# Modulation rows of an adaLN block: from one-column matmuls on TensorE to float32 sums on VectorE

## The chip, the cores and the metric

The kernel runs on one core of a Trainium2 chip. The metric is the device time of one execution in microseconds (us). Each kernel was executed several times; I quote the median of its runs. Where it matters I give the mean clock that the chip granted to TensorE beside the time, as time/clock.

Engines are abbreviated as in the profile: PE is TensorE (the matmuls), PEld its weight loads, DVE VectorE, ACT ScalarE, POOL GpSimd. "L255" in a profile line is line 255 of that kernel's source, so the same function has different line numbers before and after.

## The reference, cut to what matters

```python
# S=2048, D=1024, F=3584, 32 heads of 32
mod = silu(c) @ w_mod                      # (1, 6*1024): six rows
sa, ca, ga, sb, cb, gb = mod.reshape(6, D)
h = layernorm(x) * (1 + ca) + sa
x = x + ga * attention(h, wqkv, wo)        # linear attention, phi(t) = where(t > 0, t+1, exp(t)) + 1e-6
h = layernorm(x) * (1 + cb) + sb
x = x + gb * ((silu(h @ w_gate) * (h @ w_up)) @ w_down)
```

The rows `sa` and `ca` are needed at once. The four "late" rows are not: `ga` is wanted when `wo` is used, `sb` and `cb` at the second layernorm, `gb` at the very end.

## The kernel before

The 2048 rows of x are handled in four row blocks of 512. The program is one hand-made list of stages, each of eight "groups" of eight 128x512 matmuls. A label names a group: `("K", 2, 0)` is the first group of the K projection of row block 2. Code hung on a label with `put` is emitted behind that group. The early stages run in this order:

K0 → V0 → KV0 → Q0 → K1 → V1 → KV1 → K2 → V2 → KV2 → K3 → V3 → KV3 → Q1, Q2, Q3 and attention output → gate/up (GU) and down (D).

A KV stage is two halves of 16 matmuls, and the first group of the next stage stands between the halves, so that PE has something to do while the last V group is evacuated.

```python
def nextbank():                     # five PSUM banks, in turn
    b = bank[state["b"]]; state["b"] = (state["b"] + 1) % 5; return b

def phi_to(dst, acc):               # K and Q groups: one ACT and two DVE operations
    nc.scalar.activation(out=e, in_=acc, func=ACT.Exp)
    nc.vector.tensor_scalar(out=e, in0=e, scalar1=1.0, scalar2=PHI_EPS, op0=ALU.min, op1=ALU.add)
    nc.vector.scalar_tensor_tensor(out=dst, in0=acc, scalar=0.0, in1=e, op0=ALU.max, op1=ALU.add)

def v_group(sc_, t, h):             # V groups: evacuated by ACT alone
    ...                             # eight matmuls into acc
    nc.scalar.copy(out=v_c[...], in_=acc)

def ln(st):                         # layernorm of one 128-row tile
    ln_stats(st)                    # DVE statistics, GpSimd power
    ln_xn(st, True)                 # GpSimd normalises
    nc.sync.dma_start_transpose(out=M4[...], in_=xns[st % 6])

def modulate(sc_, cc, sT, c1T):     # h * (1 + ca) + sa on DVE, 128x512
    nc.vector.tensor_scalar(out=h, in0=h, scalar1=c1T[:, cc:cc+1], scalar2=sT[:, cc:cc+1], ...)

def late_mm(i):                     # half a late row: 32 one-column matmuls on PE
    for ii in range(4):
        for j in range(8):
            nc.tensor.matmul(mps[:, col:col+1], lhsT=wml[i % 3][:, j, ii*P:(ii+1)*P], rhs=scT[:, j:j+1], ...)

def late_bc(q, dst):                # a row broadcast to 128 partitions, for ga and gb
    ...                             # DVE writes rep, PE multiplies it with the identity, ACT copies

for sc in (2, 3):                   # row blocks 2 and 3: four tiles, then two times four modulates
    put_ln(sc, [("K", sc-1, 1), ("K", sc-1, 3), ("K", sc-1, 5), ("K", sc-1, 7), ("V", sc-1, 4), ("V", sc-1, 6)])
lab = [(k, sc, i) for sc in (1, 2) for k in ("K", "V") for i in (2, 6)]
for i in range(8):
    put(lab[i], lambda i=i: late_mm(i))
...
put(("K", 2, 0), lambda: nc.sync.dma_start(out=wo, in_=wo_v))     # 2 MB
```

Of the kernel before, what the change touches and what calls it, by code (L numbers as in the profile page):

```python
# [8 lines left out]
ACT = mybir.ActivationFunctionType  # L9
ALU = mybir.AluOpType  # L10
BF16 = mybir.dt.bfloat16
F32 = mybir.dt.float32
# [9 lines left out]
def kernel(  # L22
# [13 lines left out]
    nc = tc.nc  # L36
    P = nc.NUM_PARTITIONS
    _, S, D = A_x.shape
# [3 lines left out]
    DC = D // P  # L42
# [4 lines left out]
    STC = SCW // P  # L47
    NB = 512
    NH = D // NB
# [13 lines left out]
    wo_v = A_wo.rearrange("(c p) n -> p c n", p=P)  # L63
# [3 lines left out]
    wm_v = w_mod.rearrange("(p j) n -> p j n", j=DC)  # L67
    c_v = c.rearrange("o (p j) -> p (o j)", j=DC)

    const = ctx.enter_context(tc.tile_pool(name="const", bufs=1))  # L70
# [6 lines left out]
    bank = [psum.tile([P, NB], F32, name=f"bank{i}") for i in range(8)]  # L77
# [3 lines left out]
    M3 = const.tile([P, 16384], BF16, name="M3")  # L81
    M4 = const.tile([P, NSC, DC, SCW], BF16, name="M4")
    M5 = const.tile([P, 14336], BF16, name="M5")
# [3 lines left out]
    def view(region, off, shape, dtype=BF16):  # L87
        n = 1
        for s_ in shape:
            n *= s_  # L90
        w = n * (2 if dtype == F32 else 1)
        ap = region[:, off:off + w]
        if dtype == F32:
            ap = ap.bitcast(F32)
        if len(shape) == 2:
            ap = ap.rearrange("p (a b) -> p a b", a=shape[0])
        elif len(shape) == 3:
            ap = ap.rearrange("p (a b c) -> p a b c", a=shape[0], b=shape[1])
        return ap
# [8 lines left out]
    wml = [view(M3, 4096 * (1 + i), [DC, NB]) for i in range(3)]  # L108
# [9 lines left out]
    wo = view(M6, 0, [DC, D])  # L118
    x1rs = [view(M6, 2048 * i, [D], F32) for i in range(2)]
    obs = [view(M6, 4096 + 1024 * i, [D]) for i in range(2)]  # L120
    yts = [view(M6, 6144 + 1024 * i, [NB], F32) for i in range(2)]
    xs = [view(M7, 1024 * i, [D]) for i in range(6)]
    xns = [view(M7, 6144 + 1024 * i, [D]) for i in range(6)]
    wgs = [view(M7, 4096 * i, [DC, FBW]) for i in range(3)]
# [11 lines left out]
    def load_x(st):  # L136
        nc.sync.dma_start(out=xs[st % 6], in_=x2[st * P:(st + 1) * P, :])
# [22 lines left out]
    load_wk(6, 7)  # L160
    load_wk(7, 8)

    zt = const.tile([P, NB], BF16, name="zt")
    nc.vector.memset(zt[:], 0.0)
    ident = const.tile([P, P], BF16, name="ident")
    make_identity(nc, ident[:])
    neg_half = const.tile([P, 1], F32, name="neg_half")
# [4 lines left out]
    saT = const.tile([P, DC], BF16, name="saT")  # L172
    ca1T = const.tile([P, DC], BF16, name="ca1T")
    sbT = const.tile([P, DC], BF16, name="sbT")
    cb1T = const.tile([P, DC], BF16, name="cb1T")
    m1 = const.tile([P, 6, DC], BF16, name="m1")
    ga_bc = const.tile([P, D], BF16, name="ga_bc")
    gb_bc = const.tile([P, D], BF16, name="gb_bc")
    KVZ = const.tile([P, HG, KVW], BF16, name="KVZ")
    rep = const.tile([P, DC, P], BF16, name="rep")  # L180

    scT = const.tile([P, DC], BF16, name="scT")
    nc.scalar.activation(out=scT[:], in_=c_sb[:], func=ACT.Silu)

    def warm(n):
        for _ in range(n):
            nc.tensor.matmul(bank[7][:], lhsT=zt[:, 0:P], rhs=zt[:], start=True, stop=True)


    stat = {}  # L190
# [25 lines left out]
    def ln(st):  # L216
        ln_stats(st)
        ln_xn(st, True)
        sc_, t = divmod(st, STC)
        nc.sync.dma_start_transpose(out=M4[:, sc_, :, t * P:(t + 1) * P], in_=xns[st % 6])  # L220

    def modulate(sc_, cc, sT, c1T, c0=0, c1=SCW):
        h = M4[:, sc_, cc, c0:c1]
        nc.vector.tensor_scalar(out=h, in0=h, scalar1=c1T[:, cc:cc + 1], scalar2=sT[:, cc:cc + 1],  # L224
                                op0=ALU.mult, op1=ALU.add)


    state = {"b": 0}

    def nextbank():  # L230
        b = bank[state["b"]]
        state["b"] = (state["b"] + 1) % 5
        return b
# [51 lines left out]
                                    in1=mask[:, P:KVW].unsqueeze(1).to_broadcast([P, n, HPC]), op=ALU.mult)  # L285


    LATE = [(2, "ga"), (3, "sb"), (4, "cb"), (5, "gb")]

    def load_late(i):  # L290
        q, kb = LATE[i // 2][0], i % 2
        k0 = q * D + kb * NB
        nc.sync.dma_start(out=wml[i % 3], in_=wm_v[:, :, k0:k0 + NB])

    def late_mm(i):
        q, kb = LATE[i // 2][0], i % 2
        mps = bank[7][:, 320 + 8 * q:328 + 8 * q]
        for ii in range(NB // P):
            col = kb * (NB // P) + ii
            for j in range(DC):  # L300
                nc.tensor.matmul(mps[:, col:col + 1], lhsT=wml[i % 3][:, j, ii * P:(ii + 1) * P],  # L301
                                 rhs=scT[:, j:j + 1], start=False, stop=(j == DC - 1), skip_group_check=True)
        if kb == 1:
            nc.vector.tensor_copy(out=m1[:, q, :], in_=mps[:, 0:DC])

    def late_fin(q):
        if q == 3:
            nc.vector.tensor_copy(out=sbT[:], in_=m1[:, 3, :])
        elif q == 4:
            nc.vector.tensor_scalar_add(out=cb1T[:], in0=m1[:, 4, :], scalar1=1.0)  # L310
        else:
            nc.vector.tensor_copy(out=rep[:], in_=m1[:, q, :].unsqueeze(2).to_broadcast([P, DC, P]))

    def late_bc(q, dst):
        for h in range(NH):
            b = nextbank()
            for i in range(NB // P):
                cc = h * (NB // P) + i
                nc.tensor.matmul(b[:, i * P:(i + 1) * P], lhsT=rep[:, cc, :], rhs=ident[:], start=True, stop=True)
            nc.scalar.copy(out=dst[:, h * NB:(h + 1) * NB], in_=b[:])  # L320


    def tr0(st):
# [25 lines left out]
    def mod_pair(p):  # L349
        mod_mm(0, 2 * p, 2 * p + 2)  # L350
        mod_mm(1, 2 * p, 2 * p + 2)
        mod_rows(2 * p, 2 * p + 2)

    warm(21)
    for st in range(STC):
        ln_stats(st)
    mask = const.tile([P, KVW], BF16, name="mask")
# [6 lines left out]
    ln_xn(0, False)  # L364
    tr0(0)
    warm(3)
    ln_xn(1, False)
    tr0(1)
# [13 lines left out]
    for cc in range(2):  # L382
        modulate(0, cc, saT, ca1T, 0, 2 * P)
    G = [(t, h) for t in range(STC) for h in range(NH)]
    for cc in range(2):
        for g in range(4):
            kmm(bank[g], 0, G[g][0], G[g][1], cc)
        if cc == 0:
            tr0(3)
            tr0_evac(3)  # L390
            for c_ in range(2):
                modulate(0, c_, saT, ca1T, 2 * P, 4 * P)
    for cc in range(2):
        for g in range(4, 7):
            kmm(bank[g], 0, G[g][0], G[g][1], cc)
        if cc == 0:
            mod_pair(1)
            for c_ in range(2, 4):
                modulate(0, c_, saT, ca1T)
# [25 lines left out]
    def put(label, *fns):  # L425
        after.setdefault(label, []).extend(fns)
# [143 lines left out]
                    add(("D", st, 1), lambda st=st: d_mm(st, 1))  # L570


    def put_ln(sc_, labels):
        for t in range(STC):
            put(labels[t], lambda t=t: ln(sc_ * STC + t))
        for i in range(2):
            put(labels[STC + i],
                lambda i=i: [modulate(sc_, cc, saT, ca1T) for cc in range(4 * i, 4 * i + 4)])

    put_ln(1, [("V", 0, 1), ("V", 0, 2), ("V", 0, 3), ("V", 0, 4), ("Q", 0, 2), ("Q", 0, 3)])  # L580
    for sc in (2, 3):
        put_ln(sc, [("K", sc - 1, 1), ("K", sc - 1, 3), ("K", sc - 1, 5), ("K", sc - 1, 7),
                    ("V", sc - 1, 4), ("V", sc - 1, 6)])
    put(("V", 0, 6), lambda: load_late(0), lambda: load_late(1), lambda: load_late(2))
    put(("V", 0, 7), lambda: [load_x(st) for st in range(8, 12)])
    put(("V", 1, 7), lambda: [load_x(st) for st in range(12, 16)])


    lab = [(k, sc, i) for sc in (1, 2) for k in ("K", "V") for i in (2, 6)]
    for i in range(8):  # L590
        put(lab[i], lambda i=i: late_mm(i))
        if i + 3 < 8:
            put(lab[i], lambda i=i: load_late(i + 3))
    put(("K", 1, 7), lambda: late_fin(2))
    put(("V", 1, 1), lambda: late_bc(2, ga_bc))
    put(("V", 1, 7), lambda: late_fin(3))
    put(("K", 2, 0), lambda: nc.sync.dma_start(out=wo, in_=wo_v))
    put(("K", 2, 7), lambda: late_fin(4))
    put(("V", 2, 7), lambda: late_fin(5))
    put(("K", 3, 1), lambda: late_bc(5, gb_bc))  # L600
    for cc in range(DC):
        put(("V", 3, cc), lambda cc=cc: nc.vector.tensor_tensor(out=wo[:, cc, :], in0=wo[:, cc, :], in1=ga_bc[:],
                                                               op=ALU.mult))


# [78 lines left out]
```

## Time and profile before

| | before |
|---|---|
| median time (four runs) | 847.24 us |
| span of the profiled run (a fifth one, 847.73 us), mean PE clock | 845.9 us, 1.00 |
| PE busy | 833.4 us, 99% |
| DVE busy | 322.9 us, 38% |
| ACT busy | 144.8 us, 17% |

The profile's first part (busy time and share of the span, with the number of instructions) and its fourth (the chain of work that ended last, by engine), before:

```profile
PE 833.4 (99%) x4368; PEld 395.7 (47%) x4452; DVE 322.9 (38%) x617; ACT 144.8 (17%) x270; POOL 78.8 (9%) x142
...
PE 95%; DVE 1%; SPq 1%; DMA 1%; issue 1%; ACT 0%; DVEq 0%
```

PE is the bound, and hardly ever waits.

The timeline of PE before, through the V1 and KV1 stages (start, duration, engine, source line, operation, count; in brackets the idle time before and what ended it):

```profile
74.10 0.94 PE L301 MATMUL bank<-scT,M 128*128 128x1 bf16 x32
74.90 1.89 PE L242 MATMUL bank<-M,M 128*128 128x512 bf16 x7
76.62 3.62 PE L257 MATMUL bank<-M,M 128*128 128x512 bf16 x16
81.22 0.62 PE L319 MATMUL bank<-ident,rep 128*128 128x128 bf16 x8 [0.98 <-DVE rep L312]
...
93.64 1.07 PE L274 MATMUL bank<-M 128*128 128x129 bf16 x16
94.55 1.89 PE L242 MATMUL bank<-M,M 128*128 128x512 bf16 x8
96.28 1.07 PE L274 MATMUL bank<-M 128*128 128x129 bf16 x16
```

L242, L257 and L274 are K, V and KV matmuls. L301 is a batch of 32 one-column products for half a late row: the group behind it starts 0.80 us after it. L319 is the broadcast of `ga`; PE even waits 0.98 us for the data. At 94.55 stands K2's first group, 1.73 us of work, between the halves of KV1.

The timeline of DVE before, in the same stretch:

```profile
80.48 0.68 DVE L312 COPY rep<-m 128x1024 bf16<-128x1024 bf16 x1
90.06 2.67 DVE L224 TENSOR_SCALAR M<-M,ca1T,saT 128x512 bf16<-128x512 bf16 x8 [8.89 <-DMA M<-M]
```

DVE has nothing to do for 8.89 us, waiting for the last DMA transpose of row block 2, and then modulates all of the block in 2.67 us. The eight modulated slices are ready at 92.7, before K2 wants them at 94.55. DVE's wait costs nothing, because no V group needs DVE.

### The profile page before, as it was taken

Reading aid. Unit: us, or ns where it says so; the run is one execution under the profiler, and the core shown is the slowest. Engines: PE = TensorE matmul, PEld = TensorE weight load, DVE = VectorE, ACT = ScalarE, POOL = GpSimd, SP = SyncE. Lnnn points to the kernel's source line nnn. Section 1 sums busy time; section 2 is a strip of 40 time slices with the busy share of each in tenths; the row PEclk is TensorE's granted clock in tenths of the full one; section 3 lists DMA queues with packets and bytes.
Section 4 is the critical chain, followed back from the end, with each engine's and each line's share of the span. In section 5 each row is a group of like instructions: output and inputs, shape, how many; then the busy total and the mean of one; then the engine's idle time right before and its main releaser. Section 6 shows DMA issues by size and latency. Waiting matters only on the chain.

```text
span 845.9 us, 10893 instructions
## 1 busy us (share of the span) xinstructions
PE 833.4 (99%) x4368; PEld 395.7 (47%) x4452; DVE 322.9 (38%) x617; ACT 144.8 (17%) x270; POOL 78.8 (9%) x142
## 2 busy tenths in 40 slices
PE   8999999999999999999999999999999999999998
PEld 4454554544444444444444444444444444444444
DVE  5667455488755655421111222211122122112222
ACT  4333223322211111111110001111000111100000
POOL 2124130013122323100000000000000000000000
PEclk9999999999999999999999999999999999999999
DMA  9995982056489888778875215555322555201220
GB/s 290 307 242 132 273 196 56 1 125 159 95 220 228 209 220 212 187 227 259 246 232 176 69 60 163 150 150 149 106 75 70 154 154 158 82 18 63 76 69 26
DMA packets 203763, 128.65 MB, mean 152 GB/s; under 512 B 50496, under 2 KB 189888, under 8 KB 203712
## 3 DMA queue, kind: packets, MB, share of 16 engines
q1 hardware_dynamic: 162864, 98.58, 41.0%
q10 hardware_dynamic: 38544, 20.98, 11.2%
q0 software_dynamic: 2304, 8.39, 2.6%
q8 instruction: 35, 0.57, 0.3%
q14 instruction: 16, 0.13, 0.0%
HBM read 103.81 MB, written 12.58 MB: 138 GB/s over the span
## 4 chain that ended last, share of the span: by engine, by line
PE 95%; DVE 1%; SPq 1%; DMA 1%; issue 1%; ACT 0%; DVEq 0%
PE bank L511 23%; PE bank L530 23%; PE bank L505 23%; PE bank L462 7%; PE bank L265 6%; PE bank L257 6%; PE bank L242 5%; DMA M<-in_w_mod_dram 1%; PE bank L435 1%; PE bank L274 1%; PE bank L301 1%; SPq L145 1%; SPq L142 1%; DVE stats L196 0%; DVE M L239 0%
## 5 line engine op out<-in xcount | busy, mean ns | idle before, releaser
L511 PE MATMUL bank<-M,M 128*128 128x512 bf16 x881 | 210.4, 379 | 0.8
L505 PE MATMUL bank<-M,M 128*128 128x512 bf16 x871 | 209.7, 379 | 1.3
L513 DVE TENSOR_TENSOR M<-bank,e 128x512 bf16<-128x512 f32 x112 | 77.4, 691 | 275.1 <-PE bank L511 265.7
L530 PE MATMUL bank<-M,M 128*128 128x512 bf16 (+1 forms) x687 | 146.9, 370 | 0.6
L508 ACT ACTIVATE e<-bank 128x512 f32<-128x512 f32 x112 | 66.8, 597 | 439.7 <-PE bank L505 415.7
L530 PEld LDWEIGHTS <-M 128*128 128x128 bf16 x924 | 90.4, 98 | 103.3
L511 PEld LDWEIGHTS <-M 128*128 128x128 bf16 x896 | 87.7, 98 | 105.7
L505 PEld LDWEIGHTS <-M 128*128 128x128 bf16 x896 | 87.3, 98 | 103.8
L534 DVE TENSOR_TENSOR M<-bank,gb_bc 128x512 f32<-128x512 f32 (+1 forms) x33 | 22.3, 675 | 149.2 <-PE bank L530 135.3
L242 PE MATMUL bank<-M,M 128*128 128x512 bf16 x244 | 57.3, 379 | 1.6 <-DVE M L224 0.6
L462 PE MATMUL bank<-M,M 128*128 128x512 bf16 x254 | 57.8, 379 | 0.1
L265 PE MATMUL bank<-M,M 128*128 128x512 bf16 x250 | 56.7, 379 | 0.3
L257 PE MATMUL bank<-M,M 128*128 128x512 bf16 x250 | 56.2, 379 | 0.3
L237 ACT ACTIVATE e<-bank 128x512 f32<-128x512 f32 x64 | 37.8, 598 | 101.9 <-PE bank L265 48.4
L530 PE MATMUL bank<-M 128*128 128x512 bf16 x219 | 50.7, 379 | 0.3
L239 DVE SCALAR_TENSOR_TENSOR M<-bank,e 128x512 bf16<-128x512 f32 x64 | 44.3, 692 | 3.7
L238 DVE TENSOR_SCALAR e<-e 128x512 f32<-128x512 f32 x64 | 27.7, 433 | 40.5 <-ACT e L237 40.5
L462 PEld LDWEIGHTS <-M 128*128 128x128 bf16 x256 | 25.0, 98 | 29.7
L257 PEld LDWEIGHTS <-M 128*128 128x128 bf16 x256 | 24.7, 98 | 29.0
L265 PEld LDWEIGHTS <-M 128*128 128x128 bf16 x256 | 24.6, 98 | 27.8
L242 PEld LDWEIGHTS <-M 128*128 128x128 bf16 x256 | 24.0, 97 | 28.8 <-DVE M L224 2.1
L464 DVE TENSOR_TENSOR M<-bank,M 128x512 f32<-128x512 f32 x32 | 22.1, 690 | 14.5 <-PE bank L462 14.3
(66 smaller groups left out, 334.1 us busy)
## 6 DMA issues: line engine op xcount, KB each, us to landing
M<-in_B_w_gate_dram SPq DMA_DIRECT2D x56, 512.0 KB, 3.9
M<-in_B_w_up_dram SPq DMA_DIRECT2D x56, 512.0 KB, 5.0
M<-in_w_mod_dram SPq DMA_DIRECT2D x8, 1024.0 KB, 7.4
x_scratch<-M POOLq DMA_DIRECT2D x16, 512.0 KB, 5.6
M<-x_scratch ACTq DMA_DIRECT2D x16, 512.0 KB, 3.4
M<-in_B_w_down_dram SPq DMA_DIRECT2D x6, 1024.0 KB, 7.9
M<-in_A_x_dram SPq DMA_DIRECT2D x16, 256.0 KB, 6.6
M<-in_w_mod_dram SPq DMA_DIRECT2D x8, 512.0 KB, 8.1
```

Of the source, the lines that this page charges most:

```text
L237: nc.scalar.activation(out=e[:], in_=acc, func=ACT.Exp)
L238: nc.vector.tensor_scalar(out=e[:], in0=e[:], scalar1=1.0, scalar2=PHI_EPS, op0=ALU.min, op1=ALU.add)
L239: nc.vector.scalar_tensor_tensor(out=dst, in0=acc, scalar=0.0, in1=e[:], op0=ALU.max, op1=ALU.add)
L242: nc.tensor.matmul(acc[:], lhsT=M4[:, sc_, cc, t * P:(t + 1) * P], rhs=wk[:, cc, h * NB:(h + 1) * NB], start=(cc == 0), stop=(cc == DC - 1))
L257: nc.tensor.matmul(acc[:], lhsT=M4[:, sc_, cc, t * P:(t + 1) * P], rhs=wv[:, cc, h * NB:(h + 1) * NB], start=(cc == 0), stop=(cc == DC - 1))
L265: nc.tensor.matmul(acc[:], lhsT=wq[:, cc, qc * P:(qc + 1) * P], rhs=M4[:, sc_, cc, :], start=(cc == 0), stop=(cc == DC - 1))
L462: nc.tensor.matmul(acc[:], lhsT=oTs[st % 3][:, cc, :], rhs=wo[:, cc, hs], start=(cc == 0), stop=(cc == DC - 1))
L505: nc.tensor.matmul(g_ps[:], lhsT=wg_blk[:, cc, fs], rhs=M4[:, sc_, cc, :], start=(cc == 0), stop=(cc == DC - 1))
L508: nc.scalar.activation(out=sg[:], in_=g_ps[:], func=ACT.Silu)
L511: nc.tensor.matmul(u_ps[:], lhsT=wu_blk[:, cc, fs], rhs=M4[:, sc_, cc, :], start=(cc == 0), stop=(cc == DC - 1))
L513: nc.vector.tensor_tensor(out=gus[sc_][:, f, :], in0=u_ps[:], in1=sg[:], op=ALU.mult)
L530: nc.tensor.matmul(y_ps[:, 0:w], lhsT=gus[sc_][:, f, t * P:(t + 1) * P], rhs=wd(f)[:, c0:c1], start=(f == 0), stop=(f == FC - 1))
```

## The change

Its intent: take the late rows off the bound engine. Each half row is summed on DVE in float32 (one multiply, seven multiply-adds), split there into a high and a low bfloat16 part, and only that is multiplied with ones on PE, half a stage later, from two buffers. To make room on DVE, the modulation of row blocks 2 and 3 moves to ACT. Four of the 21 zero matmuls at the start (`warm`) go.

The diff, cut to its core:

```diff
+    def modulate_act(sc_, cc):
+        h = M4[:, sc_, cc, :]
+        nc.scalar.activation(out=h, in_=h, func=ACT.Identity, scale=modF[:, 1, cc:cc+1], bias=modF[:, 0, cc:cc+1])
...
-    def late_mm(i):                      # 32 one-column matmuls
+    def late_sum(acc, kb, slot, js):
+        for j in js:
+            if j == 0:
+                nc.vector.tensor_scalar_mul(out=dst, in0=wml[slot][:, 0, :], scalar1=scF[:, 0:1])
+            else:
+                nc.vector.scalar_tensor_tensor(out=dst, in0=wml[slot][:, j, :], scalar=scF[:, j:j+1], in1=dst,
+                                               op0=ALU.mult, op1=ALU.add)
+    def late_split(acc, kb, hl):
+        nc.vector.tensor_copy(out=hl[:, 0, :], in_=src)
+        nc.vector.tensor_tensor(out=hl[:, 1, :], in0=src, in1=hl[:, 0, :], op=ALU.subtract)
+    def late_cols(q, kb, hl):            # sb, cb: 8 one-column products with ones per half row
+    def late_bc(kb, hl, dst):            # ga, gb: 2 products 128x512 with ones per half row
...
-    warm(21)
+    warm(17)
...
     for sc in (2, 3):
         put_ln(sc, [("K", sc-1, 1), ("K", sc-1, 3), ("K", sc-1, 5), ("K", sc-1, 7),
-                    ("V", sc-1, 4), ("V", sc-1, 6)])                    # DVE, 2 x 4 modulates
+                    ("V", sc-1, 3), ("V", sc-1, 4), ("V", sc-1, 5), ("V", sc-1, 6)])   # ACT, 4 x 2
...
+    for i, (q, sc) in enumerate(((GA, 1), (SB, 2), (CB, 3))):
+        for kb in range(2):
+            sums(accA, kb, (2*i + kb) % 3, [("V", sc, 4*kb + k) for k in range(4)])   # beside the V groups
+            # split at ("V", sc, 4) or ("K", sc+1, 0); products at ("K", sc+1, 4)
-    put(("K", 2, 0), lambda: nc.sync.dma_start(out=wo, in_=wo_v))
+    put(("K", 2, 3), lambda: nc.sync.dma_start(out=wo, in_=wo_v))
+    # gb: sums, split and products in the second gate/up stage
     for cc in range(DC):
-        put(("V", 3, cc), ...)           # wo *= ga
+        put(("K", 3, cc), ...)
```

## The prediction

> **What bounds the kernel.** The chain of waits is 95% PE; PE is busy 833.4 of 845.9 us at a granted clock of 1.00. DVE is 38% busy, ACT 17%. So only what PE executes, or waits for, counts. Nearly all that changes before 160 us lies in the K and V stages, eight groups of eight 128x512 matmuls each (1.73 us a group).
>
> **Removed from PE.** 256 one-column matmuls (L301): each batch of 32 pushes the next group back by 0.80 us in the timeline, 8 x 0.80 = 6.4 us. The broadcast through identity: 0.98 us idle plus 0.45 us for ga (81.2), 0.45 us for gb. Together about 8.3 us. Four of the zero matmuls go too, but the third transpose (11.4 us) waits for ACT and the stage to 21 us for a w_mod transfer: no gain.
>
> **Added to PE.** Eight 128x512 products with ones (8 x 0.216 = 1.7 us) and 32 one-column ones (0.8 us). Net on paper: 6 us less, 841 us.
>
> **Added to DVE.** 64 sums of 512 elements, about 0.69 us each like 128x512 operations in the trace, and eight splits of about 1.15 us: some 50 us. Three quarters of it falls into V stages 1 to 3 (about 12.5 us each), where DVE now does 7.2 us or less of work in 15 to 17; the last part falls into the second gate/up stage, 20% busy. Removed: 16 modulates of 0.41 us. DVE stays just inside its time.
>
> **What eats the gain.** Modulation of row blocks 2 and 3 moves to ACT, between the evacuations of V groups. It needs the last DMA transpose. Before, DVE waited for it 8.9 us (until 90.06) and 5.5 us (until 120.41), harming nobody, then did eight modulates in 2.67 us. ACT, in order, now blocks there, V evacuations behind it. [...]
> The transposes should land at about 87.2 (no 1 MB row transfer ahead of them now[...]). ACT then ends at about 95.2; K stage 2's first group ends there, where PE alone would be done at 91.5: 3.7 us lost. Second round: landing about 120.8, ACT done 128.8, about 3 us lost. KV of block 2 then ends at about 129.9, as before (129.8). Later, PE only gains work: 0.4 us of columns in K3, 0.4 in Q1, less 0.45 of gb, and 0.86 us of gb in gate/up.
>
> **Prediction: 847.5 us, 8 in 10 within 844.5 to 850.5.** Faster by over 2%: 0.01; within 2%: 0.97; slower by over 2%: 0.02.
>
> **Right if:** PE waits of 3 to 4 us appear at about 90 to 95 and again (2 to 4) at 124 to 129, released by ACT; ACT waits for DMA some 4 us twice; the sums take 0.65 to 0.75 us. **Wrong if:** the transposes land 2 us or more earlier (then 843 to 845), or ACT modulates are cheaper; if these gaps lower the PE clock, or DVE's backlog reaches K groups, 851 and more.

The sum came to 847.5 us. Two of its terms are cut, because no trace or run of this case stood behind them: how long a 512-wide modulate takes on ACT, from which eight with four evacuations came to 8.0 us (87.2 to 95.2, and 120.8 to 128.8), and 1 us put on the last GpSimd normalise, inside the landing at 87.2. So the 3.7 and "about 3 us lost", which follow from them, had no measured base; what after showed in their place is under points 2, 3 and 5 of "Why the prediction was right or wrong".

## The result, and the profile after

| | before | after |
|---|---|---|
| median time | 847.24 us | 848.85 us |
| each run after, with PE clock | | 849.52/.996, 849.43/.996, 846.61/1.0, 848.27/.998 |
| PE busy | 833.4 us | 831.4 us |
| DVE busy | 322.9 us | 370.5 us |
| ACT busy | 144.8 us | 155.8 us |

The ratio of after to before is 1.0015, with a 95% interval of 0.9995 to 1.0035: the same. (A ratio is the mean time of one kernel's runs over that of the other's of the same rounds, so not quite the ratio of the medians quoted.) The profiled execution is the 849.52 us run; its span is 847.6 us. Both outputs are correct.

The lines of the profile after that answer to the first two before (busy time, and the chain by engine):

```profile
PE 831.4 (98%) x4135; PEld 390.7 (46%) x4216; DVE 370.5 (44%) x678; ACT 155.8 (18%) x287; POOL 79.7 (9%) x143
...
PE 89%; DVE 3%; DMA 2%; ACT 1%; issue 1%; SPq 1%; POOL 1%; DVEq 0%; ACTq 0%; POOLq 0%
```

PE has fewer instructions, but its share of the chain fell from 95% to 89%: the end of the program now goes back, in places, through DVE, GpSimd, a DMA and ACT. The timeline of PE after, over the same stages, shows one such place (L255, L270 and L287 are K, V and KV matmuls):

```profile
60.63 13.98 PE L255 MATMUL bank<-M,M 128*128 128x512 bf16 x63
74.44 13.98 PE L270 MATMUL bank<-M,M 128*128 128x512 bf16 x62
88.26 1.07 PE L287 MATMUL bank<-M 128*128 128x129 bf16 x16
89.17 1.03 PE L255 MATMUL bank<-M,M 128*128 128x512 bf16 x4
90.46 0.39 PE L255 MATMUL bank<-M,M 128*128 128x512 bf16 x1 [0.27 <-ACT M L238]
91.17 0.39 PE L255 MATMUL bank<-M,M 128*128 128x512 bf16 x1 [0.32 <-ACT M L238]
92.35 0.39 PE L255 MATMUL bank<-M,M 128*128 128x512 bf16 x1 [0.79 <-ACT M L238]
93.06 0.39 PE L255 MATMUL bank<-M,M 128*128 128x512 bf16 x1 [0.31 <-ACT M L238]
93.28 1.65 PE L287 MATMUL bank<-M 128*128 128x129 bf16 x16
```

The first two stages are now solid: 13.98 us each without an interruption. KV1 begins at 88.26 instead of 93.64, so PE is 5.4 us ahead. Then K2's first group, which is 1.73 us of work, takes from 89.17 to 93.28, one matmul at a time, each waiting for an ACT modulate. About 2.4 us are lost.

The timeline of ACT after, in that stretch (L238 are the modulates, L273 the evacuations of V groups):

```profile
85.81 1.52 ACT L238 ACTIVATE M<-M,modF 128x512 bf16<-128x512 bf16 x2 [3.62 <-DMA M<-M]
87.24 0.56 ACT L273 CAST M<-bank 128x512 bf16<-128x512 f32 x1
87.70 1.52 ACT L238 ACTIVATE M<-M,modF 128x512 bf16<-128x512 bf16 x2
...
91.01 0.57 ACT L273 CAST M<-bank 128x512 bf16<-128x512 f32 x1
91.47 1.53 ACT L238 ACTIVATE M<-M,modF 128x512 bf16<-128x512 bf16 x2
```

ACT waits 3.62 us for the last transpose, and the V evacuations queue up behind that wait: the next one starts at 87.24, 5.63 us after the one at 81.61, where those before came every 1.73 us (PE is not held up by them: all its waits here are for modulates, L238). Then eight modulates and four evacuations take 7.6 us, from 85.81 to 93.46, where DVE took 2.67 us for its eight. The last slice is ready at 93.0; PE wanted it at about 90.7.

That is still not all. The view of windows of one microsecond after (columns: window and its length, then busy share and count of PE, PEld, DVE, ACT and POOL, then the granted PE clock, the DMA share and GB/s) shows what the clock did behind the gaps:

```profile
92.00:93.00 1.00, 0.39 (x1) 0.10 (x1) 0.96 (x2) 1.00 (x3) 0.00 (x0) 1.00 1.03 395
93.00:94.00 1.00, 0.94 (x11) 0.80 (x12) 0.51 (x1) 0.99 (x2) 0.00 (x0) 0.86 0.84 324
94.00:95.00 1.00, 1.00 (x10) 0.88 (x9) 0.78 (x2) 0.08 (x1) 0.00 (x0) 0.50 0.19 53
95.00:96.00 1.00, 1.00 (x3) 0.30 (x2) 0.97 (x3) 0.00 (x0) 0.00 (x0) 0.50 0.87 268
96.00:97.00 1.00, 1.00 (x3) 0.45 (x3) 0.40 (x1) 0.00 (x0) 0.00 (x0) 0.50 1.08 374
97.00:98.00 1.00, 0.85 (x5) 0.40 (x5) 0.00 (x0) 0.15 (x1) 0.00 (x0) 0.93 0.99 350
```

Right behind the gaps the clock is halved for 3.4 us. Adding up what is missing from 1.00 over the windows gives 1.7 us of lost PE time. "PE busy" hides this: from 95.3 to 97.0, at clock 0.50, the 128x512 matmuls of L255 were busy for 634 ns each in the mean, against 379 ns from 98 to 101, at 1.00; so PE looks full with three in a window instead of five or six.

The same happens once more, at the start of K3: the transposes land at 120.1, ACT waits 3.52 us, PE's gaps lie between 124.6 and 127.4 and cost 2.3 us, and from 127.9 to 131.3 the clock is down again. So the two rounds cost (2.4 + 1.7) + (2.3 + 1.7) = 8.1 us.

### A ledger: where V3 begins

One point in the timeline turned out to say nearly everything: the start of stage V3, behind both of these places. The timelines of PE have these lines, before and then after:

```profile
142.36 13.98 PE L257 MATMUL bank<-M,M 128*128 128x512 bf16 x63
```

```profile
142.72 13.98 PE L270 MATMUL bank<-M,M 128*128 128x512 bf16 x63
```

From there to the end of the span, before takes 845.9 − 142.36 = 703.5 us and after 847.6 − 142.72 = 704.9 us. The difference, 1.3 us, is what the change adds on PE later on: the columns of `cb` and the broadcast of `gb` (0.4 and 0.86 us by the prediction's sum). The table gives the same numbers for every kernel, with the experiments that follow.

| kernel | V3 begins, us | span, us | V3 to end, us |
|---|---|---|---|
| before | 142.36 | 845.9 | 703.5 |
| e2 (before, ACT modulates) | 142.96 | 846.6 | 703.6 |
| e5 (before, 17 zero matmuls) | 141.97 | 845.7 | 703.7 |
| after | 142.72 | 847.6 | 704.9 |
| e11 (after again) | 140.97 | 845.9 | 704.9 |
| e3 (gaps filled with zeros) | 139.88 | 844.8 | 704.9 |
| e4 (no sums) | 139.70 | 844.6 | 704.9 |
| e6 (layernorm earlier) | 140.00 | 844.9 | 704.9 |
| e8 (sums spread) | 145.47 | 850.4 | 704.9 |
| e1 (DVE modulates) | 138.66 | 847.5 | 708.8 |
| e7 (DVE modulates, no sums) | 134.63 | 839.5 | 704.9 |
| e9 (layernorm earlier, loads later) | 134.63 | 839.5 | 704.9 |
| e10 (layernorm earlier still) | 134.71 | 839.6 | 704.9 |
| e12 (e10 again, with a clock drop at the start) | 136.50 | 841.4 | 704.9 |

So, with the one exception of e1, everything is decided before V3. Against e9, which has the same PE work and no gaps, after is 142.72 − 134.63 = 8.1 us late: just the 8.1 us added up above.

### The profile page after: what moved, and what is told of

Same layout as the page of the kernel before. It is cut to its first block, busy times and chain, and to the rows that moved or that the text cites. A ratio compares the mean times of both kernels' runs of the same rounds, so it can differ in the third digit from the quotient of the medians. Undisturbed runs are those within 1.5% of the kernel's fastest.

```text
span 847.6 us, 10495 instructions
## 1 busy us (share of the span) xinstructions
PE 831.4 (98%) x4135; PEld 390.7 (46%) x4216; DVE 370.5 (44%) x678; ACT 155.8 (18%) x287; POOL 79.7 (9%) x143
## 4 chain that ended last, share of the span: by engine, by line
PE 89%; DVE 3%; DMA 2%; ACT 1%; issue 1%; SPq 1%; POOL 1%; DVEq 0%; ACTq 0%; POOLq 0%
PE bank L550 23%; PE bank L531 23%; PE bank L525 22%; PE bank L482 7%; PE bank L278 6%; PE bank L255 3%; PE bank L270 3%; DVE M L252 1%; DVE stats L205 1%; DMA M<-in_w_mod_dram 1%; ACT M L238 1%; PE bank L455 1%; PE bank L287 1%; DMA M<-M 1%; SPq L149 1%
## 5 line engine op out<-in xcount | busy, mean ns | idle before, releaser
L255 PE MATMUL bank<-M,M 128*128 128x512 bf16 x247 | 60.2, 389 | 5.0 <-ACT M L238 3.3
L270 PE MATMUL bank<-M,M 128*128 128x512 bf16 x251 | 55.6, 379 | 0.3
L252 DVE SCALAR_TENSOR_TENSOR M<-bank,e 128x512 bf16<-128x512 f32 x64 | 44.3, 692 | 3.7
L255 PEld LDWEIGHTS <-M 128*128 128x128 bf16 x256 | 25.0, 100 | 36.4 <-ACT M L238 6.0
L270 PEld LDWEIGHTS <-M 128*128 128x128 bf16 x256 | 25.0, 98 | 30.2
L313 DVE SCALAR_TENSOR_TENSOR M<-M,scF,M 128x512 f32<-128x512 bf16 x42 | 33.2, 791 | 1.5
```

The lines of the kernel that those rows point to most:

```text
L255: nc.tensor.matmul(acc[:], lhsT=M4[:, sc_, cc, t * P:(t + 1) * P], rhs=wk[:, cc, h * NB:(h + 1) * NB], start=(cc == 0), stop=(cc == DC - 1))
L270: nc.tensor.matmul(acc[:], lhsT=M4[:, sc_, cc, t * P:(t + 1) * P], rhs=wv[:, cc, h * NB:(h + 1) * NB], start=(cc == 0), stop=(cc == DC - 1))
L313: nc.vector.scalar_tensor_tensor(out=dst, in0=wml[slot][:, j, :], scalar=scF[:, j:j + 1], in1=dst, op0=ALU.mult, op1=ALU.add)
```

## The experiments

The theories that the expectations name:

- **A**: the gain is eaten where ACT waits for the last transpose and then modulates too slowly for K2's and K3's first groups. Take the modulates off ACT, or let the transposes land earlier, and the gain appears.
- **B**: the rival. DVE, with the sums, is full; its backlog delays the K evacuations, the statistics and with them the transposes. Take the sums away and the gain appears.
- **C**: short gaps lower the PE clock, which costs nearly as much again as the gaps (in after, at K2, 1.7 us behind 2.4).
- **D**, formed after the first runs: A and B are two limits one behind the other, and lifting one only uncovers the other.

Experiments e1 to e4 ran on one chip (before there: 847.32), e5 to e8 on a second, e9 and e10 on a third (before: 847.38), e11 and e12 on a fourth (before: 847.59). All outputs were correct, apart from e4 and e7. Their outputs are wrong, which doesn't matter for the times.

### e1: modulates back on DVE

```diff
 # after, with
-            for i in range(4):
-                put(labels[STC + i], lambda i=i: [modulate_act(sc_, cc) for cc in (2*i, 2*i + 1)])
+        for i in range(2):
+            put(labels[STC + i], lambda i=i: [modulate(sc_, cc, saT, ca1T) for cc in range(4*i, 4*i + 4)])
-                    ("V", sc-1, 3), ("V", sc-1, 4), ("V", sc-1, 5), ("V", sc-1, 6)])
+                    ("V", sc-1, 4), ("V", sc-1, 4)])
```

> The changed kernel with one part undone: row blocks 2 and 3 are modulated on DVE again, all eight cc after V group 4, behind the first half sum. Theory A (ACT blocks on the last transpose and then needs about 7.6 us for eight modulates and four evacuations, which holds up PE): the two waits of PE for ACT, near 90 to 93 and 124 to 127 us, vanish, no clock drop follows, and the time falls to about 843.5 us (842 to 845.5); some of the paper gain of 6 us stays lost because DVE then carries about 32 us of work per K and V pair against 29.5 on PE. Rival B (the sums fill DVE, and DVE is what PE really waits for): with 2.7 us more DVE work per block the time rises to 850 us or more.

Measured: 849.11 us (849.4/.995, 849.13/.996, 848.93/.998, 849.08/.996), ratio 1.0022 [1.0007, 1.0037]. Theory A alone missed by more than 5 us; the rival's figure was nearly right. The timeline of PE in e1 tells why:

```profile
88.95 1.89 PE L255 MATMUL bank<-M,M 128*128 128x512 bf16 x8
...
98.49 1.24 PE L339 MATMUL bank<-M,ones 128*128 128x512 bf16 x4
101.96 7.02 PE L255 MATMUL bank<-M,M 128*128 128x512 bf16 x24 [2.23 <-DVE M L252]
...
161.75 0.54 PE L326 MATMUL bank<-ones,M 128*128 128x1 bf16 x16 [2.12 <-DVE KVZ L297]
```

The gaps in K2's first group are gone: its eight matmuls run in one piece. But now PE waits 2.23 us for a DVE evacuation (L252) and 2.12 us for KVZ, which DVE builds. Both waits are followed by the clock at 0.50 (102 to 105, and 163 to 167), 1.7 us lost each. The first puts V3 at 138.66, which is 4.0 us behind e7; the second is why V3 to the end takes 3.9 us longer. Theory D comes from this run.

### e2: before, with the modulates on ACT and no sums

```diff
 # before, with modulate_act as in the change (blocks 2 and 3)
-                    ("V", sc-1, 4), ("V", sc-1, 6)])
+                    ("V", sc-1, 3), ("V", sc-1, 4), ("V", sc-1, 5), ("V", sc-1, 6)])
```

> The kernel before with only one part of the change: modulation of row blocks 2 and 3 on ACT, between V evacuations (zeros moved to another buffer for space); no sums on DVE, late rows still on PE. Theory A: PE now waits for ACT at the start of K stages 2 and 3; with transposes landing near 90 and 120 us as before, ACT ends about 98 and 130 us, and the loss is about 2 us without and up to 5 us with clock drops: 849 to 852 us. Rival B (sums are to blame): without the sums nothing is lost, 847.2 us.

Measured: 848.31 us (847.96 to 848.44, clock 0.999 to 1.0), ratio 1.0012 [0.9997, 1.0027]; before on this chip 847.32. (To make space, the zeros of `warm` moved to another buffer, as in the change.) Theory A's 849 to 852 was missed: the sign is as expected, though the interval includes no difference, and the size is smaller. There are two gaps of 0.37 and 0.31 us at 96, none in the second round. PE is not ahead in this kernel, so K2 wants the slices later and ACT is nearly in time. The loss on ACT is therefore not a constant price of the move: it is paid where PE arrives earlier.

### e3: the gaps filled with zero matmuls

```diff
 # after; in K2,0 and K3,0 only
             kmm(acc, sc_, t, h, cc)
+            if sc_ in (2, 3) and (t, h) == (0, 0) and cc in (3, 4, 5, 6):
+                for _ in range(3 if cc == 5 else 2):
+                    nc.tensor.matmul(acc[:], lhsT=zt[:, 0:P], rhs=zt, start=False, stop=False)
```

> The changed kernel, with nine matmuls of zeros added into the accumulator of the first group of K stages 2 and 3, in the gaps in which PE waits for ACT (result unchanged). Theory C (gaps of about 2 us of idle time in 3.5 us lower the granted clock to 0.5 for about 3.5 us, and this makes runs differ by 1.7 us per drop, 846.6 with none, 849.5 with two): clock 1.000 in every run, all within 846.4 to 847.2 us. Rival: the clock drop has another cause; then the runs keep spreading from 846.6 to 849.5 with clocks of 0.996 to 1.000.

In each of the two groups, nine zero matmuls that add nothing to the sum are put where PE would wait anyway. Measured: 846.43 us (846.1 to 846.68, clock 0.999 to 1.0), ratio 0.9989 [0.9972, 1.0006]. The windows of e3, the same columns as above:

```profile
94.00:95.00 1.00, 1.00 (x15) 0.76 (x13) 0.53 (x2) 0.32 (x1) 0.00 (x0) 1.00 0.17 64
95.00:96.00 1.00, 1.00 (x6) 0.42 (x5) 0.97 (x3) 0.00 (x0) 0.00 (x0) 1.00 0.73 218
```

K2's first group still takes as long (89.41 to 93.52), but the clock stays at 1.00, and the kernel is always near after's undropped run (846.61) and 2.4 us below after's median. This is what theory C expects, but it is not proof by itself: e4, on the same chip and with its gaps unfilled, had no drop in its four runs either. What ties the drops to the gaps is set out under "When the clock drops", after the experiments.

### e4: no sums

```diff
 # after; the 42 multiply-adds of ga, sb and cb dropped, loads, splits and products kept
-            else:
+            elif q == GB:
                 nc.vector.scalar_tensor_tensor(out=dst, ...)
```

> The changed kernel without the 42 multiply-adds of the ga, sb and cb rows on DVE (only the first product of each half row is kept; the result is wrong on purpose). Theory A: the transposes land only about 0.7 us earlier[...], the ACT wait and the PE gaps stay, time 845 to 848.5 us with or without clock drops. Rival B (the sums' 11 us per V stage on DVE are what costs): the gaps of PE vanish and the time falls to about 841 to 842 us.

Measured: 846.56 us (846.42 to 847.29, clock 0.999 to 1.0), ratio 0.9993 [0.9979, 1.0008]. The timelines of ACT and of PE in e4:

```profile
85.93 1.52 ACT L238 ACTIVATE M<-M,modF 128x512 bf16<-128x512 bf16 x2 [3.66 <-DMA M<-M]
```

```profile
90.58 0.39 PE L255 MATMUL bank<-M,M 128*128 128x512 bf16 x1 [0.31 <-ACT M L238]
91.28 0.39 PE L255 MATMUL bank<-M,M 128*128 128x512 bf16 x1 [0.31 <-ACT M L238]
92.47 0.39 PE L255 MATMUL bank<-M,M 128*128 128x512 bf16 x1 [0.80 <-ACT M L238]
93.17 0.39 PE L255 MATMUL bank<-M,M 128*128 128x512 bf16 x1 [0.31 <-ACT M L238]
```

The transposes land at 85.93, as before the cut (85.81; the 0.7 us expected here was an estimate), and PE's gaps in K2's first group are the same (0.31, 0.31, 0.80, 0.31 us); so they are in K3's (0.35, 0.32, 0.80, 0.31 us). So the sums are not what makes ACT late, and theory B alone is false. In this profile the clock did not drop behind the same gaps (1.00 in every window from 92 to 99 and from 126 to 131 us), which no setting of this kernel explains (see "When the clock drops").

### e5: before, with 17 zero matmuls at the start

```diff
-    warm(21)
+    warm(17)
```

> The kernel before with 17 zero matmuls at the start in place of 21, nothing else. The prediction said no gain. The changed kernel is however 0.6 us earlier at the start of the V stage (31.2 against 31.8 us). If the zero matmuls do that, this runs 0.4 to 0.7 us faster (846.6 to 846.9); if it is luck of a transfer, it stays at 847.2.

Measured: 847.52 us (847.29 to 847.71, all at clock 1.0). Before on the same chip had runs of two kinds: 847.23 and 847.61 at 1.0, and five of 848.99 to 849.72 at 0.998. The printed ratio, 0.9987, mixes the two. At equal clock there is no difference, as predicted.

### e6: layernorm of blocks 2 and 3 earlier

```diff
 # after
-        put_ln(sc, [("K", sc-1, 1), ("K", sc-1, 3), ("K", sc-1, 5), ("K", sc-1, 7),
+        put_ln(sc, [("K", sc-1, 0), ("K", sc-1, 1), ("K", sc-1, 3), ("K", sc-1, 5),
```

> The changed kernel with the layernorm of row blocks 2 and 3 one or two K groups earlier (K groups 0, 1, 3, 5 in place of 1, 3, 5, 7), nothing else. Theory A: the last transposes land 2 to 4 us earlier, ACT is through with the modulates before PE needs them; the gaps at 90 and 124 us shrink below 1 us. Theory D (DVE is loaded from 64 to 162 us almost without a pause, and once the ACT waits are gone its backlog becomes the floor, as the run with modulates on DVE showed at 101 and 161 us): part of the gain comes back as a wait of PE for banks in K stage 2, about 1 to 2 us, and the time ends at 843 to 845.5 us. A alone: 841 to 842.5.

Measured: 846.79 us (846.8/.998, 845.14/1.0, 847.07/.998, 846.78/.998), ratio 0.9974 [0.9958, 0.9991] against the mixed runs of that chip. Missed upward by the median; the one run without a drop, 845.14, is at the upper end of theory D's 843 to 845.5. The profiled run's drop is at the start (12.1 to 15.5 us), not in K2 or K3. The first round's gaps are gone. In the second round the transposes still landed at 119.07 and PE had gaps of 0.57, 0.32, 0.80 and 0.32 us; the 2 MB load of `wo`, issued at 108.3 and landed at about 118.0, was under way before the last one. Two waits of 1.13 and 0.34 us for DVE in K2 came up instead. Moving only one producer was half a remedy.

### e7: modulates on DVE, and no sums

```diff
 # e1 and e4 together
```

> The changed kernel with both undone: modulates of blocks 2 and 3 on DVE, and no multiply-adds of the ga, sb and cb rows (wrong on purpose). It fills the table of two by two: ACT modulates with sums 848.8 (846.6 without clock drops), DVE modulates with sums 849.1, ACT modulates without sums 846.6. Theory D (two limits lie behind each other: ACT's wait and DVE's backlog; either alone eats the gain): with both gone the paper gain appears, 841 to 842.5 us, clock 1.000. If something else limits, it stays above 845.

Measured: 841.41 us (841.43, 841.38 and 841.39 at clock 1.0; 841.62/.997), ratio 0.9915 [0.9901, 0.993] against the mixed runs; against before's two runs at clock 1.0 it is about 6 us. With e1, e4 and after this is a two-by-two table:

| | sums on DVE | no sums |
|---|---|---|
| modulates on ACT | after: 848.85 (846.6 without a clock drop) | e4: 846.56 |
| modulates on DVE | e1: 849.11 | e7: 841.41 |

The four cells do not all come from one chip, but before was the same within 0.4 us on each, at clock 1.0. Lifting either limit alone gains nothing beyond the clock. Lifting both gains what the change was meant to gain. That is theory D, shown; what kind of limit the second one is, e9 tells.

### e8: the sums spread over more stages

```diff
 # after; layernorm as in e6; and
-    put(("V", 1, 7), lambda: [load_x(st) for st in range(12, 16)])
+    put(("V", 1, 1), lambda: [load_x(st) for st in range(12, 16)])
+    # half rows summed at Q0,4-7 | V1,0-3 | V1,4-7 | V2,0-3 | V2,4-7 | V3,0-3
+    # products moved, most of them into the V stages; splits and loads moved too
```

> A candidate for a better kernel: layernorm of blocks 2 and 3 early as in the run above, the first half row summed in Q stage 0 where DVE has 5 us free, the five others in V stages 1, 1, 2, 2, 3, products with ones moved out of K stage 2 into V stages, x rows loaded earlier. Theory D: both limits are eased, so 841 to 843 us with a clock of 1.000; if D is wrong about the backlog, no better than the run with the early layernorm.

Measured: 853.31 us (852.28 to 853.44, clock 0.994 to 0.998), ratio 1.0056 [1.0039, 1.0072], again against the mixed runs. A clear miss, and the slowest kernel. Q groups need DVE for every evacuation, as K groups do. Sums put among them stand in DVE's program order ahead of urgent operations, and the backlog runs into K1 and V1: PE waits 0.26, 0.93, 0.34 and 0.34 us for L252 between 71 and 83 us. Later PE waits for a split, block 3's last transpose lands at 123.1 and ACT waits 7.06 us. In before, DVE was busy for 12.47 of the 15.4 us of K1 and for 9.86 of the 15.6 us of KV0 and Q0, but for only 7.21 of the 17.0 us of V1.

### e9: layernorm earlier, and the transfers that stood in its way later

```diff
 # after; layernorm at K 0, 1, 3, 5 as in e6; and
-    put(("V", 0, 6), lambda: load_late(GA, 0, 0), lambda: load_late(GA, 1, 1), lambda: load_late(SB, 0, 2))
+    put(("V", 0, 7), lambda: load_late(GA, 0, 0), lambda: load_late(GA, 1, 1), lambda: load_late(SB, 0, 2))
-            put(("K", sc+1, 4) if sc < 3 else ("Q", 1, 2),
+            put((("KV", 1, 1), ("V", 2, 3))[kb] if q == GA else ("K", sc+1, 4) if sc < 3 else ("Q", 1, 2),
-    put(("K", 2, 3), lambda: nc.sync.dma_start(out=wo, in_=wo_v))
+    put(("V", 2, 3), lambda: nc.sync.dma_start(out=wo, in_=wo_v))
```

> The run with the early layernorm, with its three leftovers mended: the 2 MB load of wo, which delayed the last transpose of block 3 by about 4 us there (landing 119.1 us), is issued in V stage 2 after the transposes; the two products with ones for ga leave K stage 2, where they took two of the five banks (1.5 us of PE waiting for DVE); the x rows of block 2 are loaded ahead of the modulation rows. DVE work is unchanged. If theory A with its second half, theory D, is complete: no wait of PE for banks, one gap of at most 1.5 us at the start of K stage 3, clock 1.000, 841 to 842.5 us. If DVE's load as such were the limit, it stays at 844 us or more.

Measured: 841.5 us (841.44, 841.25 and 841.56 at clock 1.0; 843.2/.998), ratio 0.9934 [0.9917, 0.995]. Nothing is undone here: the sums stay on DVE, the modulates on ACT. The timelines of ACT and of PE in e9:

```profile
82.49 1.52 ACT L238 ACTIVATE M<-M,modF 128x512 bf16<-128x512 bf16 x2 [0.25 <-DMA M<-M]
```

```profile
88.30 1.07 PE L287 MATMUL bank<-M 128*128 128x129 bf16 x16
89.21 1.89 PE L255 MATMUL bank<-M,M 128*128 128x512 bf16 x8
90.93 1.07 PE L287 MATMUL bank<-M 128*128 128x129 bf16 x16
```

ACT's wait for the transpose shrank from 3.62 to 0.25 us (and from 3.52 to 0.73 in the second round), and K2's first group runs in one piece. This is the version that gains. It also shows that the second limit was not DVE's load as such: the sums are all there and DVE is busy for 68.4 us of the 74 from 88 to 162, more than in after, and still PE waits for no evacuation in K2. So it was a matter of what stands in front of the evacuations in K2. e9 makes three changes at once on top of e6 (the row loads, the products for `ga`, and `wo`); how much each of them is worth was not measured.

### e10: layernorm earlier still

```diff
 # e9, with
-        put_ln(sc, [("K", sc-1, 0), ("K", sc-1, 1), ("K", sc-1, 3), ("K", sc-1, 5),
+        put_ln(sc, [("K", sc-1, 0), ("K", sc-1, 1), ("K", sc-1, 2), ("K", sc-1, 4),
```

> The same with the layernorm of blocks 2 and 3 one K group earlier still (K groups 0, 1, 2, 4). The transposes land about 1.1 us earlier, and the rest of the gap at K stage 3 closes, but the phi operations behind it come later: equal to the run before it or 0.3 to 1 us faster if ACT's wait was what was left, 0.5 us or more slower if the banks are (PE then waits for DVE in K stages).

Measured: 841.5 us (841.42 to 841.53, all at clock 1.0), ratio 0.9927 [0.9913, 0.9942]. ACT no longer waits for a transpose at all, and the time is the same as e9's. PE has no gap left there that an earlier landing could close.

### e11 and e12: after and the better version on one chip, five rounds

> The changed kernel again, unaltered, beside the kernel before and the candidate on one chip. By theory A and C: single runs between 846.4 and 849.7 us, in steps of about 1.7 us, each step with 0.002 less mean clock; a median within 0.25% of the kernel before.

> The candidate (early layernorm, late wo load, products with ones out of K stage 2) again, unaltered: 841.3 to 841.7 us with clock 1.000 in nearly all runs, 0.6 to 0.8% faster than the kernel before and 0.6 to 1.0% faster than the changed kernel on the same chip.

After again (e11): 847.77 us (847.77/.998, 846.22/1.0, 848.0/.998, 848.06/.998, 847.46/1.0), ratio 0.9998 [0.9984, 1.0011]. One of these runs, 847.46 at clock 1.0, does not fit the expected steps of 1.7 us. The better version again (e12, the kernel of e10): 841.6 us (843.27/.998, 841.6/.997, 841.73, 841.58 and 841.4 at 1.0), ratio 0.9933 [0.992, 0.9945]. It beats both kernels, by about 0.7%, or 6 us: little, but outside the interval of either.

The profiled run of e12 happens to be its slow one, and shows another place where the clock drops. First the timeline of PE, then one of the windows, in e12:

```profile
21.11 0.55 PE L361 MATMUL bank<-scT,M 128*128 128x1 bf16 x16 [1.22 <-DMA M<-in_w_mod_dram]
```

```profile
22.00:23.00 1.00, 1.00 (x3) 0.29 (x2) 0.80 (x3) 0.00 (x0) 0.00 (x0) 0.50 1.20 292
```

A wait of 1.22 us for the `w_mod` transfer is followed by half clock from 21.7 to 25.1 us. Before has the same wait of 1.22 us at 21.27. It probably explains before's own occasional runs of 849 us at 0.998, but I have no trace of such a run: that is argued, not shown.

### When the clock drops

The traces show where the same gaps were followed by a lower clock and where not. Each whole drop in them lasts 3.41 us. Windows of 0.2 us give the starts: 93.72 and 127.86 in after, 34.14 us or ten drop lengths apart; 101.98 and 163.42 in e1, 61.44 us or eighteen, which makes 3.413 us each. e11 has one drop at 126.35 and another at 846.57, behind the end of the span, 720.22 us or 211 times 3.413 us later. In these three executions the drops thus began whole steps of 3.413 us apart; I read that as a grid, so that a gap can lie inside one step of it or across two. From a trace's drop one can count back to the step before each gap. (e4 and e6 have no drop near K2 or K3; there I counted from one at 844.94 and one at 12.12.)

| trace, stage | step of the grid, us | PE idle in it, us | clock in the next step |
|---|---|---|---|
| after, K2 | 90.31 to 93.72 | 1.57 | 0.50 |
| after, K3 | 124.44 to 127.86 | 1.61 | 0.50 |
| e11, K2 | 88.81 to 92.22 | 1.39 | 1.00 |
| e11, K3 | 122.94 to 126.35 | 1.51 | 0.50 |
| e4, K2 | 90.60 to 94.01 | 1.42 | 1.00 |
| e4, K3 | 121.32 to 124.73 and the next | 0.89 and 0.89 | 1.00 |
| e6, K3 | 124.76 to 128.17 | 1.12 | 1.00 |
| e1, K2 | 98.56 to 101.98 | 2.23 | 0.50 |
| e1, before its second drop | 160.00 to 163.42 | 1.75 | 0.50 |

The windows of e11, behind K2's gaps and behind K3's, show both outcomes in one run:

```profile
95.00:96.00 1.00, 0.95 (x5) 0.45 (x5) 0.97 (x3) 0.00 (x0) 0.00 (x0) 1.00 1.00 322
127.00:128.00 1.00, 0.78 (x5) 0.51 (x5) 0.89 (x3) 0.00 (x0) 0.00 (x0) 0.50 1.26 285
```

In the steps listed, every one with 1.51 us or more of idle PE was followed by half clock, and none with 1.42 us or less. In these traces that ties the drops to the gaps, and which runs drop to how the grid happens to lie. Among the small matmuls of the start less was enough: there the drops of e12 and e6 followed steps with only 1.22 and 1.04 us idle. All this was read from the kept traces afterwards; no run set the gaps' place on purpose.

## Why the prediction was right or wrong

The prediction was 847.5 us, "within 2%". It was measured at 848.85, inside the range, and the class is right. The mechanism is right too; the number owes something to luck (points 3 and 4). Point by point:

1. **PE's saving: right.** With nothing in the way (e9), V3 begins 142.36 − 134.63 = 7.7 us earlier than before. The prediction's sum for that stretch is 8.3 us removed, less 0.9 for `ga`'s products and 0.4 for `sb`'s columns, so 7.0; most of the rest is an earlier start of V0 in the traces (31.23 in e9 and 31.19 in after, against 31.77 before), behind a shorter wait for the same `w_mod` transfer (0.91 us in after, 1.22 before).
2. **What eats it: right in mechanism.** ACT waits for DMA twice, 3.62 and 3.52 us ("some 4 us twice"), and PE waits for ACT where it was said. The transposes landed at 85.8 and 120.1, against 87.2 and 120.8. Two modulates in a row took 1.52 us; eight with four evacuations took 7.6 us, against the 8.0 between 87.2 and 95.2 in the prediction.
3. **The size of the gaps: too large.** The terms "3.7 us lost" and "about 3 us lost" measured 2.4 and 2.3 us, since the transposes landed earlier and ACT was a little quicker than assumed. The first is below the 3 to 4 us under "Right if".
4. **The clock: left out of the sum.** It was named only among the risks: "if these gaps lower the PE clock". That is the step that was wrong. The risk was also priced too high, at "851 and more". Two drops of 1.7 us each were in the profiled run; they separate after's 849.5 from its 846.6. Here two errors of opposite sign met: 2.0 us too much for the gaps, 3.4 us too little for the clock, in the runs that drop twice. A third error hides in the addition: 129.9 against 129.8 for KV of block 2, and then 0.4 + 0.4 − 0.45 + 0.86, make 1.3 us more than before, or 848.5 us, not 847.5. From 848.5, less 2.0 for the gaps, one comes to 846.5, where the runs without a drop are (846.61, and 846.22 in e11). That 847.5 is within 1.4 us of the median is thus partly luck.
5. **"DVE stays just inside its time": too mild.** The sums took 0.752 us each in the median (0.79 in the mean, with `ga`, `sb` and `cb`), above the point estimate of 0.69 and just outside the stated 0.65 to 0.75. A split took 423 ns for the cast and 692 ns for the subtraction, 1.12 us against 1.15. One sum beside a GpSimd normalise (after, 81.69) took 1571 ns, and that normalise 1.62 us, where the three before it took 1.32. DVE was busy 64.2 of the 74 us from 88 to 162, against 37.4 before. It was a second limit, hidden behind ACT's: with the modulates back on DVE it ate the whole gain (e1), and with ACT's first wait out of the way PE waited 1.5 us for it (e6).
6. **Later stages: right.** "PE only gains work" after KV of block 2: 1.3 us from V3 to the end, in every version of the change but e1.
7. **Fewer zero matmuls: no gain, as said** (e5).

On the clock, the traces show drops of 3.41 us, whole steps of 3.413 us apart within one execution, at other times in another ("When the clock drops"). What stays open: how much idle time is enough among small matmuls, and what the mean clock of a run says by itself. Two runs, 841.62/.997 (e7) and 841.6/.997 (e12), were no slower than their fellows at 1.0, and neither was profiled; a drop behind the end of the span, as e11 has one, costs nothing.

## What to carry to other kernels

Work moved off the bound engine is gained only if the engines that feed its next operation can keep up in that stage: look at the place where the bound engine will arrive earlier, and at who has to be earlier for it; a mean load of 17% or 38% does not answer that. Where an operation that waits for a late transfer feeds the bound engine, the producers and the competing transfers can be moved rather than the operation (here layernorm, three loads and `wo`, with the products for `ga`). When one experiment shows no gain, a second limit may stand behind the first: lift both before dropping the theory, and count the clock behind PE's gaps as well as the gaps (here 1.7 us for each drop).
